# Attention, then a maxout FFN, on one core: one ring of five tiles for outputs and maxima, and new prices for transfers in the planner

## The chip, the cores and the metric

The kernel runs on one core of one Trainium2 chip. The metric is device microseconds of one launch, as the median of three runs: 785.98 us before the change (785.86 to 788.97).

## What is computed

```python
scores = scale * q @ k.T                        # 8 batches, 8 heads, 576 rows, head_dim 64, fp32
bias   = -(cum[:, None] - cum[None, :])         # cum = cumsum(max(s, 0)), per head
scores = where(causal, -1e9, scores + minimum(bias, 0))
attn   = softmax(scores); y = attn @ v          # then heads side by side: x is 4608 x 512
h      = max(x @ w1, x @ w2, x @ w3)            # w1, w2, w3: 512 x 768
out    = h @ w_out                              # w_out: 768 x 512
```

## The kernel before

Nothing in this program is written in the order in which an engine runs it. Every step (a group of matmuls, an eviction, a transfer) is added to a `Plan` with its buffers, a key (its rank) and, for each engine that may do it, a price in ns. `Plan.run` then plays the whole kernel through as a list scheduler with these prices, and the order in which it starts the steps is the order in which they are written for each engine's queue. On the chip each engine runs its queue in that order and waits in place for what a step needs. So a price is no delay by itself: it only decides which step stands ahead of which. A step with a number that is too low is placed too early, and its engine waits there.

**Prices.** A compute step is `(dur, busy)`: its result counts as there after `dur`, and its engine takes the next step after `busy`. A transfer has a third number, the time for which it fills the queue's DMA: in `Plan.run` its data counts as landed at `dma + dur`, where `dma = max(dma, now + busy) + third`. `load` prices a plain transfer at 450 ns of issue, its bytes at 0.3 (300 GB/s), and a latency of 2000 ns unless the call says otherwise. DMA transposes are priced where they are added, in `one_step` and `both`.

**Rings.** `depth` says how many tiles of a kind exist. `o` (two tiles) takes the scaled output of a down projection before its store; `m1` (three tiles) takes the running maximum of the three up projections. Both are "free" rings: a step that opens a tile waits in the plan until all steps of the tile that many places earlier have ended (`room`), its store among them, and the chip waits for the same.

**Work.** Batches come in units: "split" units (first 256 rows of a batch), "rest" units (the other 320 rows) and "whole" units. A unit loads `qr`, `rv` and the spread `bias`, then for each block of 128 rows masks (POOL), takes scores (PE), adds the bias and finds the minimum (DVE), takes the exponential (ACT), splits the result in two fp16 parts (ACT, DVE) and turns them with a DMA transpose issued from SP (lines 1299, 1107 and 1116); `values` multiplies by V. The heads of one (batch, row phase) make `x`, and `experts` then does the FFN as one set: 6 times three `u` groups of 12 matmuls with `m1` (L1479, L1490, L1502, L1509, L1514), then four `d` groups of 18 matmuls (L1535), each evicted by ACT into `o` (L1554) and stored from SP (L1560). Sets have the lowest rank on PE: they fill what attention leaves.

**The start.** The weights come as 64-bit words (L477) and are made into fp16 pairs in chunks of three or six by ACT, POOL and DVE (L485, L499, L506, L599, L637). Each chunk's scale is found with a gram matmul (L527), a reduction on DVE (L540), and `power`: a clip on DVE (L425), one matmul on PE (L434) and a reduction (L442). The first set (`first_set`, batch 0) uses the raw fp32 words (L659, L689).

Of the kernel before, what the change touches and what calls it, by code (L numbers as in the profile page):

```python
# [9 lines left out]
F32 = mybir.dt.float32  # L10
# [20 lines left out]
HOLD = (3000.0, 30000.0)  # L31
# [8 lines left out]
P3 = 10  # L40
LOWP = (2, 24)
# [30 lines left out]
class Plan:  # L72
# [48 lines left out]
    def run(self):  # L121
# [16 lines left out]
        while left:  # L138
# [4 lines left out]
            while events and events[0][0] <= now:  # L143
                _, _, _, op = heapq.heappop(events)
                if op is not None and op.start is None:
                    op.due = now + HOLD[0]
                    for e in op.ways:
                        heapq.heappush(wait[e], (op.key, op.n, op))
            for e in engines:
                if free[e] > now:  # L150
                    continue
                aside, pick, kept = [], None, None
                while wait[e]:
# [7 lines left out]
                    if kept is not None and op.mode:  # L161
                        break
                    if e == "PE" and op.mode and not shape and op.due > now > HOLD[1]:
                        kept = op
                        continue
                    pick = op
# [3 lines left out]
                if pick is None:  # L170
                    pick = kept
# [42 lines left out]
def kernel(  # L214
# [34 lines left out]
        qr=2, qh=2, ql=2, rv=4, vv=2, bias=2, p=2, pr=2, tl=2, pT0=2, pT1=2, tT=2, t=5, m1=3, o=2,  # L249
        sc=6, dg=2, am=3, vs=5, ws=3, os=4, s=2, av=1, m=3,  # L250
# [5 lines left out]
    for i in "abc":  # L256
# [3 lines left out]
        m1=1280, o=1280, sc=32, am=16, vs=32, ws=32, os=4,  # L260
# [55 lines left out]
    def load(emit, key, nbytes, reads=(), writes=(), queue="SP", rate=0.3, lat=2000.0, begin=0.0):  # L316
        plan.add({queue: (lat, 450.0, nbytes / rate * 1e-3)}, emit, key, reads, writes).ready = begin
# [20 lines left out]
    load(lambda e: E[e].dma_start(out=st()[0:HB], in_=s), -1000.0, 4 * HB * S, writes=[st], queue="ACT")  # L338
# [25 lines left out]
    def spans(c0, c1):  # L364
# [36 lines left out]
        lambda e: E[e].dma_start(out=cd(), in_=cct()[0:HB]), -1000.0, 4 * HB * S, [cct], [cd], queue="ACT", lat=5500.0  # L401
# [19 lines left out]
    def power(t, key):  # L421


        def do(e):
# [8 lines left out]
            {"PE": (250.0, 250.0)},  # L433
# [11 lines left out]


# [14 lines left out]

    def weights(c):
        ids = chunks[c]
        raw = {}
        for i in ids:
            k = (i if i < RAW else i - 1) % RAW
            if i == RAW:
# [123 lines left out]
        for i in ids:  # L591
# [4 lines left out]
            k = wkey(i)  # L596
# [46 lines left out]

    def first_set(c, raw):
# [4 lines left out]
        if c < NFT:  # L649
# [3 lines left out]
            for i in range(3):  # L653
                pm = buf("m", free=True, name=f"u_plain_{c}_{i}")
                r = raw[3 * c + i]

                def up(e, r=r, pm=pm):
                    for kt in range(NKT):
                        nc.tensor.matmul(  # L659
                            pm()[:, :nq], lhsT=words(r)[0][:, kt * P:(kt + 1) * P], rhs=xb()[:, kt * nq:(kt + 1) * nq],  # L660
                            start=(kt == 0), stop=(kt == NKT - 1),
                        )

                add({"PE": (NKT * cost + 100.0, NKT * cost)}, up, 1.0e6 + 3 * c + i, [r, xb], [pm])
                h = lambda: hb()[:, c * nq:(c + 1) * nq]
                if i == 0:
                    add(
                        {"ACT": act(nq, PSI), "DVE": dve(nq)},
                        lambda e, pm=pm, h=h: nc.scalar.activation(out=h(), in_=pm()[:, :nq], func=AF.Copy)
                        if e == "ACT"  # L670
                        else nc.vector.tensor_copy(out=h(), in_=pm()[:, :nq]),
                        FIRST + 3 * c, [pm], [(hb, c)],
                    )
                else:
                    add(
                        {"DVE": dve(nq, 155.0)},
                        lambda e, pm=pm, h=h: nc.vector.tensor_tensor(
                            out=h(), in0=pm()[:, :nq], in1=h(), op=ALU.max
                        ),
                        FIRST + 3 * c + i, [pm], [(hb, c)],  # L680
                    )
            return
        hb = H0[0]
        for dt in range(NDT):
            pm = buf("m", free=True, name=f"d_plain_{dt}")

            def down(e, pm=pm, dt=dt):
# [10 lines left out]
            o = buf("o", free=True, name=f"o_plain_{dt}")  # L698
# [9 lines left out]
                FIRST, 4 * P * nq, [o], lat=1500.0,  # L708
# [27 lines left out]
    def values_in(u):  # L736
# [19 lines left out]
        if plain(u):  # L756
            return
        first, last = gs[0] == 0, gs[-1] == NP - 1
        if first:
# [9 lines left out]
            k - 4.0, [rv], [(am, col)],  # L769
        )  # L770
        if last:
            vs = VS[sk] = buf("vs")
            kk = begin[u] - (1.0 if kind == "split" else 4.0)
# [5 lines left out]
            power(vs, kk)  # L779
# [52 lines left out]
    def qk_in(u):  # L832
# [98 lines left out]
        else:  # L931
            load(spread, k - LOOK[2], 4 * P * nb_ * rows_, [cd], [bias], lat=4500.0 if u < 4 else 2500.0)
# [85 lines left out]
    def both(u, t):  # L1018
# [94 lines left out]
        for tl, tT in zip(tls, tts):  # L1113
            add(
                {"SP": (2000.0, 1250.0, 200.0)},
# [76 lines left out]
    def one_step(u, a, g, qb, t, r, pT, sp, at):  # L1192
# [103 lines left out]
        tw = lambda n: (2000.0, 1250.0, 200.0 * n)  # L1296
# [8 lines left out]
    def turned(t, qb, pt, pr, sc, ri, pT, at):  # L1305
# [14 lines left out]
        for j in range(2):  # L1320
# [9 lines left out]
            add({"PE": (350.0 * (qb + 1) + 80.0, 350.0 * (qb + 1))}, turn, t, [(pt, (qb, j)), (pr, (qb, j))], [(m, j)])  # L1330
# [113 lines left out]

    def experts(b, ph, xb, vs):
# [73 lines left out]
        os = buf("os")  # L1519
        add(  # L1520
            {"DVE": (145.0, 65.0)},
            lambda e: nc.vector.tensor_scalar(
                out=os(), in0=vs()[:, 3:4], scalar1=ENDS()[:, 2:3], scalar2=None, op0=ALU.mult
            ),
            FIRST + 100.0 * n + 17, [(vs, 3), (ENDS, 2)], [os],
        )
        for dt in range(NDT):
            pm = buf("m", free=True, name=f"d{n}_{dt}")

            def down(e, pm=pm, dt=dt, f0=0, f1=NFT):  # L1530
                k = 3 * f0
                for ft in range(f0, f1):
                    v = W[NUP + ft]().rearrange("p h (a c) -> p h a c", c=P)
                    for wt, c in ((0, 0), (0, 1), (1, 0)):
# [93 lines left out]
```

## Time and profile before

| | us |
|---|---|
| median of 3 runs | 785.98 |
| profiled execution | 784.61 |
| its span, first to last instruction | 782.6 |
| PE busy in the span | 764.8 (98%) |
| DVE, ACT, POOL busy | 573.8, 519.2, 308.3 |
| DMA, mean rate | 174 GB/s, 136.31 MB in all |

The span is what the trace shows; 2.0 us lie around it. A row of a waits view names the waiting engine and line, and behind the arrow the step that ended its idle time.

### The profile page before, as it was taken

What the parts mean: (1) busy time and instruction counts of PE and PEld (TensorE: products, weight loads), DVE (VectorE), ACT (ScalarE), POOL (GpSimd) and SP (SyncE); (2) the same over time, 40 slices, a digit from 0 to 9 for tenths busy, and PEclk for the clock granted to TensorE, in tenths of its full rate; (3) what the DMA queues carried; (4) which work ended last, traced back from release to release, by engine and by line L of the source; (5) the groups of instructions that cost most, each with busy time, mean ns of one, the idle gap of its engine ahead of it and who ended that gap; (6) DMA issues with size and microseconds to landing.
All of it is one profiled execution on the core that took longest, in us unless ns stands there. A gap on an engine that the chain in (4) does not pass through costs nothing. (4 is left out here: it accounts for less than half of the span.)

```text
span 782.6 us, 19630 instructions
## 1 busy us (share of the span) xinstructions
PE 764.8 (98%) x7189; PEld 589.6 (75%) x7189; DVE 573.8 (73%) x1691; ACT 519.2 (66%) x1369; POOL 308.3 (39%) x361
## 2 busy tenths in 40 slices
PE   7889999999999999999999899999999999999998
PEld 5677888888888877766788677667776777778875
DVE  6999898875587888888878787888787977322131
ACT  6878777871687787986887777777876977111101
POOL 4432423641355455444544364354444452011110
PEclk9999999999999999999999999999999999999999
DMA  9799778890399899998999999898989865300000
GB/s 342 245 260 242 180 169 164 176 237 18 97 207 233 199 175 214 227 215 200 225 232 207 183 192 240 241 190 198 254 210 169 208 137 100 81 1 34 28 2 34
DMA packets 241167, 136.31 MB, mean 174 GB/s; under 512 B 204080, under 2 KB 222000, under 8 KB 241072
## 3 DMA queue, kind: packets, MB, share of 16 engines
q1 hardware_dynamic: 240912, 134.78, 75.7%
q8 instruction: 56, 0.92, 0.5%
q14 instruction: 39, 0.32, 0.2%
q10 hardware_dynamic: 160, 0.30, 0.1%
HBM read 75.64 MB, written 9.58 MB: 109 GB/s over the span
## 5 line engine op out<-in xcount | busy, mean ns | idle before, releaser
L1479 PE MATMUL u<-x,w 128*128 128x320 f16 (+1 forms) x3240 | 411.3, 287 | 2.9 <-ACT o L1554 2.9
L1479 PEld LDWEIGHTS <-w 128*128 128x128 f16 x3240 | 312.6, 98 | 99.5 <-issue 17.6
L1514 POOL TENSOR_TENSOR h<-m,h 128x320 f16<-128x320 f32 (+1 forms) x90 | 69.9, 777 | 190.4 <-ACT h L1509 174.5
L1535 PE MATMUL d<-h,w 128*128 128x320 f16 (+1 forms) x1080 | 137.9, 287 | 0.1
L1502 DVE SCALAR_TENSOR_TENSOR m<-u,m 128x320 f32<-128x320 f32 (+1 forms) x180 | 82.2, 457 | 64.3 <-PE u L1479 60.1
L1535 PEld LDWEIGHTS <-w 128*128 128x128 f16 x1080 | 104.7, 98 | 30.4 <-issue 3.2
L1222 POOL TENSOR_SCALAR_AFFINE_SELECT p<-bias 128x256 f32<-128x256 f32 (+3 forms) x91 | 68.9, 770 | 120.6 <-DVE pr L1288 68.9
L1244 ACT ACTIVATE p<-p,sc 128x256 f32<-128x256 f32 (+3 forms) x182 | 98.2, 540 | 26.3 <-DVE sc L1235 25.6
L1509 ACT ACTIVATE h<-m 128x320 f16<-128x320 f32 (+1 forms) x90 | 39.4, 438 | 102.9 <-DVE m L1502 102.6
L1288 DVE SCALAR_TENSOR_TENSOR pr<-p,sc,pr 128x256 f16<-128x256 f32 (+3 forms) x182 | 100.3, 567 | 8.0 <-ACT pr L1280 7.8
L1280 ACT ACTIVATE pr<-p,sc 128x256 f16<-128x256 f32 (+3 forms) x182 | 89.3, 538 | 13.0 <-DMA pT<-pr 7.9
L961 POOL TENSOR_TENSOR ql<-qr,qh 128x256 fp32r<-128x256 f32 (+1 forms) x76 | 82.5, 1106 | 35.0 <-ACT qh L949 30.6
L1235 DVE CUSTOM_DVE_ANT_0 p<-s,p 128x256 f32<-128x256 f32 (+3 forms) x182 | 80.4, 467 | 3.7 <-POOL p L1222 2.2
L1384 PEld LDWEIGHTS <-vv 128*64 128x64 f16 x1232 | 58.6, 110 | 18.1 <-issue 10.0
L1384 PE MATMUL av<-pT,vv 128*64 128x320 f16 (+3 forms) x1104 | 70.3, 276 | 1.2 <-DVE x L1429 0.8
L1494 DVE TENSOR_SCALAR m<-u 128x320 f32<-128x320 f32 (+1 forms) x55 | 25.3, 461 | 48.2 <-PE u L1479 47.6
L1554 ACT ACTIVATE o<-d,os 128x320 f32<-128x320 f32 (+1 forms) x60 | 28.2, 498 | 47.6 <-PE d L1535 36.8
L766 DVE TENSOR_REDUCE am<-rv 128x1 f32<-128x640 f32 (+1 forms) x44 | 33.9, 777 | 13.2 <-DMA rv<-in_qkv_dram 13.0
L1222 POOL TENSOR_SCALAR_AFFINE_SELECT ha<-bias 128x1024 f32<-128x1024 f32 (+3 forms) x29 | 26.7, 926 | 41.8 <-DVE r L1288 29.8
L1244 ACT ACTIVATE ha<-ha,sc 128x512 f32<-128x512 f32 (+3 forms) x58 | 35.9, 620 | 6.5 <-DVE sc L1235 6.1
L815 DVE SCALAR_TENSOR_TENSOR vv<-rv,vs,vv 128x640 f16<-128x640 f32 (+1 forms) x44 | 39.0, 887 | 0.4
L1288 DVE SCALAR_TENSOR_TENSOR r<-ha,sc,r 128x512 f16<-128x512 f32 (+3 forms) x58 | 37.5, 660 | 2.3 <-ACT r L1280 2.2
(170 smaller groups left out, 980.1 us busy)
## 6 DMA issues: line engine op xcount, KB each, us to landing
bias<-cd SPq DMA_DIRECT2D x32, 576.0 KB, 5.0
qr<-in_qkv_dram SPq DMA_DIRECT2D x28, 480.0 KB, 5.2
rv<-in_qkv_dram SPq DMA_DIRECT2D x32, 320.0 KB, 3.8
raw<-in_w_dram SPq DMA_DIRECT2D x16, 512.0 KB, 5.7
qr<-in_qkv_dram SPq DMA_DIRECT2D x13, 512.0 KB, 6.3
bias<-cd SPq DMA_DIRECT2D x12, 512.0 KB, 5.4
out_dram<-o SPq DMA_DIRECT2D x32, 160.0 KB, 2.4
early<-in_w_dram SPq DMA_DIRECT2D x8, 512.0 KB, 7.0
```

The lines of the kernel that those rows point to most:

```text
L961: lambda e, d0=d0, d1=d1: E[e].tensor_tensor(out=lo().bitcast(F32R)[:, d0:d1], in0=raw()[:, d0:d1], in1=hi()[:, d0:d1], op=ALU.subtract),
L1222: nc.gpsimd.affine_select(out=pt()[:, 0:8 * P].rearrange("p (j n) -> p j n", j=2)[:, :, at:at + nk], in_=r["bias"]()[:, 2 * a * w:2 * (a + ...
L1235: lambda e, j=j: nc.vector.tensor_tensor_reduce(out=pj(j), in0=src(j), in1=pj(j) if masked else bias(j), scale=-SCALE, scalar=3.0e38, op0= ...
L1244: lambda e, j=j: nc.scalar.activation(out=pj(j), in_=pj(j), func=AF.Exp, scale=-1.0, bias=nm()[:, j:j + 1], accum_out=sm()[:, j:j + 1]),
L1280: lambda e, h_=h_, s_=s_, j=j: nc.scalar.activation(out=h_(), in_=s_(), func=AF.Copy, scale=ri()[:, j:j + 1]),
L1288: lambda e, h_=h_, l_=l_, s_=s_, j=j: nc.vector.scalar_tensor_tensor(out=l_(), in0=s_(), scalar=ri()[:, j:j + 1], in1=h_(), op0=ALU.mult, ...
L1384: nc.tensor.matmul(av()[j * D:(j + 1) * D, c0:nq], lhsT=lt, rhs=rt, start=(n < 2), stop=(n >= len(todo) - 2), skip_group_check=True,)
L1479: nc.tensor.matmul(pm()[:, :nq], lhsT=v[:, wt, kt, :], rhs=x(xt, kt), start=(k == 0), stop=(k == 3 * NKT - 1),)
L1502: lambda e, pm=pm, m1=m1: nc.vector.scalar_tensor_tensor(out=m1()[:, :nq], in0=pm()[:, :nq], scalar=HSC, in1=m1()[:, :nq], op0=ALU.mult, o ...
L1509: lambda e, m1=m1, ft=ft: nc.scalar.activation(out=h(0, ft), in_=m1()[:, :nq], func=AF.Copy),
L1514: lambda e, m1=m1, ft=ft: E[e].tensor_tensor(out=h(1, ft), in0=m1()[:, :nq], in1=h(0, ft), op=ALU.subtract),
L1535: nc.tensor.matmul(pm()[:, :nq], lhsT=v[:, wt, dt, :], rhs=h(c, ft), start=(k == 0), stop=(k == 3 * NFT - 1), skip_group_check=True,)
```

## The change

`o` is dropped: outputs use the ring `m1`, which is five tiles deep instead of three. The tiles keep their size, so the two kinds together take what they took before. A further ring `far` of one tile of 512 bytes is made but not used.

Transfers have new prices. Each price has now a fourth number, the time from issue to the start of the transfer (`lead`), which takes the place of the issue time in the landing, and every transfer issued through `load` and every transpose has 1500 ns (`SPARE`) added to its latency. A plain load goes from 450 + bytes/0.3 + 2000 to 1440 + bytes/0.36 + 1285 + 1500; an output store from 450 + bytes/0.3 + 1500 to 120 + bytes/0.45 + 1320 + 1500; the spread bias from 450 + bytes/0.3 + 2500 to 1590 + bytes/0.266 + 1065 + 1500. A transpose of n blocks goes from 1250 + 200 n + 2000 to 545 + 156 n + 1570 + 1500, and holds SP for 1200, 1450 or 2000 ns instead of 1250. On PE, `power`'s matmul goes from 250 to 90 ns of engine time, and the turns of the first units from 350 to 270 ns a block.

What else the diff adds is not run at the values that stand in it: `RAWX`, `D16`, `KP` and `LATE` are 0, `FAR` is 99 with 46 units, `SAME` is 0, and `HOLD2` would start at 900 us. With `SAME` 0 and a third number of 2 the new loop over PE's held steps picks as the old one does. `down_all` is the old text of the down projection, moved.

```diff
-HOLD = (3000.0, 30000.0)
+HOLD = (3000.0, 30000.0, 2)
+SAME = 0
+D16 = 0
+SPARE = 1500.0
+FAR = 99
...
                 if len(op.ways[e]) > 2:
-                    dma[e] = max(dma[e], now + busy) + op.ways[e][2]
+                    dma[e] = max(dma[e], now + op.ways[e][3]) + op.ways[e][2]
                     op.end = dma[e] + dur
...
-        qr=2, qh=2, ql=2, rv=4, vv=2, bias=2, p=2, pr=2, tl=2, pT0=2, pT1=2, tT=2, t=5, m1=3, o=2,
-        sc=6, dg=2, am=3, vs=5, ws=3, os=4, s=2, av=1, m=3,
+        qr=2, qh=2, ql=2, rv=4, vv=2, bias=2, p=2, pr=2, tl=2, pT0=2, pT1=2, tT=2, t=5, m1=5,
+        sc=6, far=1, dg=2, am=3, vs=5, ws=3, os=4, s=2, av=1, m=3,
...
-    def load(emit, key, nbytes, reads=(), writes=(), queue="SP", rate=0.3, lat=2000.0, begin=0.0):
-        plan.add({queue: (lat, 450.0, nbytes / rate * 1e-3)}, emit, key, reads, writes).ready = begin
+    def load(emit, key, nbytes, reads=(), writes=(), queue="SP", rate=0.36, lat=1285.0, begin=0.0, lead=1440.0):
+        plan.add({queue: (lat + SPARE, 400.0, nbytes / rate * 1e-3, lead)}, emit, key, reads, writes).ready = begin
...
         add(
-            {"PE": (250.0, 250.0)},
+            {"PE": (250.0, 90.0)},
             lambda e: nc.tensor.matmul(
                 gm()[:, :P], lhsT=t()[:, 1:2].bitcast(BF16)[:, 0:1].to_broadcast([P, P]), rhs=identb(), start=True,
...
-            load(spread, k - LOOK[2], 4 * P * nb_ * rows_, [cd], [bias], lat=4500.0 if u < 4 else 2500.0)
+            load(spread, k - LOOK[2], 4 * P * nb_ * rows_, [cd], [bias], lat=3000.0 if u < 4 else 1065.0, rate=0.266, lead=1590.0)
...
-                {"SP": (2000.0, 1250.0, 1600.0)},
+                {"SP": (1570.0 + SPARE, 1250.0, 1250.0, 545.0)},
...
-                {"SP": (2000.0, 1250.0, 200.0)},
+                {"SP": (1570.0 + SPARE, 1200.0, 156.0, 545.0)},
...
-        tw = lambda n: (2000.0, 1250.0, 200.0 * n)
+        tw = lambda n: (1570.0 + SPARE, 1200.0 if n < 10 else 1450.0 if n < 14 else 2000.0, 156.0 * n, 545.0)
...
-            add({"PE": (350.0 * (qb + 1) + 80.0, 350.0 * (qb + 1))}, turn, t, [(pt, (qb, j)), (pr, (qb, j))], [(m, j)])
+            add({"PE": (270.0 * (qb + 1) + 80.0, 270.0 * (qb + 1))}, turn, t, [(pt, (qb, j)), (pr, (qb, j))], [(m, j)])
...
+            o = buf("m1", free=True, name=f"o{n}_{dt}")
...
+            load(
+                lambda e, o=o, dt=dt: nc.sync.dma_start(out=outT[dt * P:(dt + 1) * P, t0:t0 + nq], in_=o()[:, :nq]),
+                FIRST, 4 * P * nq, [o], lat=1320.0, lead=120.0, rate=0.45,
+            )
```

## Rows read from the trace of the kernel before

**Rows 1.** Busy time of each engine in six stretches of the span (length, then busy us and instructions of PE, PE's weight loads, DVE, ACT and POOL, granted PE clock as a share of 2.4 GHz, DMA share, GB/s), with the sum.

```profile
0.00:20.00 20.00, 16.01 (x145) 10.64 (x145) 14.03 (x58) 13.95 (x45) 9.07 (x22) 1.00 0.95 343
20.00:120.00 100.00, 93.51 (x1007) 78.20 (x1005) 91.13 (x328) 78.58 (x226) 35.32 (x50) 1.00 0.86 213
120.00:420.00 300.00, 300.00 (x2920) 239.95 (x2918) 238.68 (x707) 222.05 (x601) 137.31 (x157) 1.00 0.87 188
420.00:520.00 100.00, 96.71 (x901) 70.60 (x894) 80.66 (x209) 75.52 (x177) 47.28 (x48) 1.00 0.98 211
520.00:660.00 140.00, 139.31 (x1266) 98.84 (x1265) 117.44 (x323) 107.70 (x274) 65.78 (x68) 1.00 0.85 189
660.00:782.00 122.00, 119.22 (x973) 91.38 (x971) 31.82 (x72) 21.40 (x48) 13.49 (x18) 1.00 0.13 33
sum 782.00, PE 764.75 PEld 589.61 DVE 573.76 ACT 519.21 POOL 308.26; mean PE 127.46 PEld 98.27 DVE 95.63 ACT 86.53 POOL 51.38
```

**Rows 2.** Pieces of the chain that ended last, near the end of the span: start, length, what (matmuls in the piece).

```profile
708.66 23.58 PE u L1479 x216
...
740.10 29.34 PE u L1479 x216
769.44 9.79 PE d L1535 x72
779.30 0.53 ACT o L1554
```

**Rows 3.** What PE waited for, over the whole span: total us, times, longest.

```profile
PE m L434 <- DVE ws L425: 3.4, 3, 1.8
PE u L1479 <- ACT o L1554: 2.9, 2, 2.1
PE m L415 <- DVE identb L361: 1.6, 1, 1.6
PE m L434 <- DVE vs L425: 1.0, 2, 0.6
PE u_plain L659 <- PE m L434: 0.9, 1, 0.9
PE av L1384 <- DVE x L1429: 0.8, 1, 0.8
...
PE m L434 <- DVE vs L776: 0.5, 1, 0.5
PE av L1384 <- DMA pT<-pr: 0.3, 1, 0.3
PE m L434 <- ACT o L1554: 0.3, 1, 0.3
```

**Rows 4.** All instructions on tile `o`: what ACT's evictions (L1554) waited for, who waited for them, and the stores' time to landing.

```profile
  PE d L1535: 36.8, 25
  DMA out_dram<-o: 8.8, 6
...
DMA to landing us min/median/max: 1.7/2.5/5.0
```

**Rows 5.** Timeline around the longer of the two PE waits: start, length, engine, line, operation.

```profile
440.51 0.86 SPq L1560 DMA_DIRECT2D out_dram<-o  x2
...
442.18 1.20 PE L1030 MATMUL s<-qr 64*64 64x256 f32 x16
...
444.97 0.84 ACT L1554 ACTIVATE o<-d,os 128x256 f32<-128x256 f32 x2 [3.65 <-DMA out_dram<-o]
...
445.49 3.42 PE L1479 MATMUL u<-x,w 128*128 128x320 f16 x24 [2.11 <-ACT o L1554]
```

**Rows 6.** Timeline around the shorter one, with SP's queue between the first two evictions and their stores.

```profile
491.67 0.95 ACT L1554 ACTIVATE o<-d,os 128x320 f32<-128x320 f32 x2 [1.02 <-PE d L1535]
492.82 0.99 SPq L753 DMA_DIRECT2D rv<-in_qkv_dram  x2
...
493.91 2.67 SPq L1299 DMA_TRANSPOSE pT<-r  x1
...
496.67 1.12 SPq L1560 DMA_DIRECT2D out_dram<-o  x2
...
499.37 0.53 ACT L1554 ACTIVATE o<-d,os 128x320 f32<-128x320 f32 x1 [1.25 <-DMA out_dram<-o]
...
499.95 0.22 PE L434 MATMUL m<-identb,vs 128*128 128x128 bf16 x1 [0.26 <-ACT o L1554]
...
500.97 1.25 PE L1479 MATMUL u<-x,w 128*128 128x320 f16 x8 [0.81 <-ACT o L1554]
```

**Rows 7.** DMA issues by destination: count, KB each, median us from issue to landing.

```profile
bias<-cd SPq DMA_DIRECT2D x32, 576.0 KB, 5.0
rv<-in_qkv_dram SPq DMA_DIRECT2D x32, 320.0 KB, 3.8
raw<-in_w_dram SPq DMA_DIRECT2D x16, 512.0 KB, 5.7
...
pT<-pr SPq DMA_TRANSPOSE x115, 4.7
```

**Rows 8.** The weight loads (L477): issue and landing (min/median/max), and who waited for them.

```profile
  POOL raw L499: 11.0, 4
  ACT early L485: 6.7, 5
  POOL early L499: 3.9, 2
...
DMA to landing us min/median/max: 3.6/6.0/9.1
```

**Rows 9.** PE groups by shape: count, then busy us, mean ns of one, and idle time before them. (The chip runs an fp32 matmul of the program as two instructions.)

```profile
L434 PE MATMUL m<-identb,vs 128*128 128x128 bf16 x14 | 3.1, 223 | 1.2 <-DVE vs L425 1.0 <-ACT o L1554 0.3
...
L1324 PE MATMUL m<-pr-8_287,p-8_238 128*128 128x128 f32 x12 | 1.9, 292 | 0.7 <-ACT bias L926 0.7
...
L1324 PE MATMUL m<-pr-2_481,p-2_427 128*128 128x128 f32 x12 | 1.6, 284 | 0.0
L434 PE MATMUL m<-identb,ws 128*128 128x128 bf16 x7 | 1.6, 225 | 4.0 <-DVE ws L425 3.4 <-DVE vs L776 0.5
```

**Rows 10.** One stretch of `u` matmuls between other PE work, in the timeline: start, length, count.

```profile
319.06 6.69 PE L1479 MATMUL u<-x,w 128*128 128x320 f16 x48
```

More of the change, by code (lines that the diff above doesn't have):

```diff
@@ L145, in run @@
                 if op is not None and op.start is None:
-                    op.due = now + HOLD[0]
+                    op.due = now + (HOLD2 if now > HOLD2[1] else HOLD)[0]
                     for e in op.ways:
@@ L160, in run @@
                         continue
[L161 to L164, printed above, removed]
+                    if e == "PE" and op.mode:
+                        kept.append(op)
+                        if shape and (op.mode == shape or not SAME):
+                            pick = op
+                            break
+                        if not shape and (len(kept) >= (HOLD2 if now > HOLD2[1] else HOLD)[2] or not op.due > now > HOLD[1]):
+                            pick = kept[0]
+                            break
                         continue
-                    pick = op
+                    pick = kept[0] if kept and shape else op
                     break
@@ L336 @@
     cct = inner("cc", 12 * S, 4 * S)
-    load(lambda e: E[e].dma_start(out=st()[0:HB], in_=s), -1000.0, 4 * HB * S, writes=[st], queue="ACT")
+    load(lambda e: E[e].dma_start(out=st()[0:HB], in_=s), -1000.0, 4 * HB * S, writes=[st], queue="ACT", lat=2000.0)
     def do(e):
@@ L400 @@
     load(
-        lambda e: E[e].dma_start(out=cd(), in_=cct()[0:HB]), -1000.0, 4 * HB * S, [cct], [cd], queue="ACT", lat=5500.0
+        lambda e: E[e].dma_start(out=cd(), in_=cct()[0:HB]), -1000.0, 4 * HB * S, [cct], [cd], queue="ACT", lat=4000.0
     )
@@ L443, in power, with far_power @@
             key, [gm], [(t, 2)],
+        )
+    def far_power(t, key, n):
+        fd = Buf(plan, f"far{n}", lambda b: dram.tile([P, 1], F32, name=f"far{n}"), "one")
+        row = buf("far", name=f"far_row{n}")
+        add(
+            {"DVE": (157.0, 75.0)},
+            lambda e: nc.vector.tensor_scalar(
+                out=t()[:, 1:2], in0=t()[:, 0:1], scalar1=2.0 ** -80, scalar2=1.0 / VSC, op0=ALU.max, op1=ALU.mult
+            ),
+            key, [(t, 0)], [(t, 1)],
+        )
+        load(lambda e: E[e].dma_start(out=fd(), in_=t()[:, 1:2]), key, 4 * P, [(t, 1)], [fd], rate=1.0e-3)
+        load(
+            lambda e: E[e].dma_start(out=row(), in_=fd().rearrange("p o -> o p").to_broadcast([P, P])),
+            key, 4 * P * P, [fd], [row],
+        )
+        add(
+            {"DVE": (282.0, 200.0)},
+            lambda e: nc.vector.tensor_reduce(out=t()[:, 2:3], in_=row(), axis=AX.X, op=ALU.max),
+            key, [row], [(t, 2)],
         )
@@ L466, in weights @@
             k = (i if i < RAW else i - 1) % RAW
-            if i == RAW:
+            if RAWX:
+                k = RAWAT[i]
+            if RAWX and i > RAW and k < 0:
+                r = buf("ql" if k == -1 else "qh", name=f"raw{i}")
+            elif i == RAW:
                 r = Buf(plan, "r6", lambda b: early3()[:, 0:2 * N], "one", inside=early3)
@@ L697, in first_set @@
             )
-            o = buf("o", free=True, name=f"o_plain_{dt}")
+            o = buf("m1", free=True, name=f"o_plain_{dt}")
             add(
@@ L755, in values_in @@
         sk = (b, kind)
-        if plain(u):
+        if plain(u) and not D16:
             return
@@ L768, in values_in @@
             ),
-            k - 4.0, [rv], [(am, col)],
+            AMK if plain(u) else k - 4.0, [rv], [(am, col)],
         )
@@ L778, in values_in @@
             )
-            power(vs, kk)
+            if u >= FAR:
+                far_power(vs, kk - 1.0, u)
+            else:
+                power(vs, kk)
             add(
@@ L1518, in experts @@
             )
[L1519 to L1534, printed above, removed]
[L1535 to L1562 removed]
+        down_all(n, t0, nq, hb, h, vs, base)
     gone = 0
```

166 lines of the change are left out of this document (119 added, 47 removed).

## Prediction

> **What bounds the kernel now.** I read the busy time by stretches first, because the stages differ. [rows 1] show PE busy for 764.75 of 782 us at full granted clock, so 17.8 us of the 782.6 us span are open. They lie in three places: 4.0 us in the first 20 us and 6.5 us from 20 to 120, where DVE is busy for 91.13 of 100 us; nothing from 120 to 420; 3.3 us from 420 to 520 and 0.7 us from 520 to 660; and 2.8 us from 660 on, plus the last 0.6 us, which are the tail. The second thing to see is whether a busy PE is a full PE. At the end, where nothing competes, 216 matmuls of 256 columns take 23.58 us and 216 of 320 columns 29.34 us [rows 2]: 109.2 and 135.8 ns each, against 106.7 and 133.3 ns for as many columns at 2.4 GHz. The change adds and removes no matmul, so this part stays; only the 17.8 us and the switches between kinds of PE work can move.
>
> Third, what PE waited for [rows 3]. The waits fall in two families. One is of the start: 3.4 us for the clip of a weight chunk's maximum, 1.6 us for the identity, and some pieces below 1 us. The other is an eviction of outputs, 2.9 us for `u` and 0.3 us for `power`'s matmul, all of it between 440 and 501 us. Fourth, why that eviction was late. ACT's evictions into `o` waited 8.8 us in six cases for a store to land [rows 4]. In the longer case [rows 5] two stores go out at 440.51, PE ends its scores at 443.4, ACT has sat idle for 3.65 us until a store has landed, evicts at 444.97, and PE goes on with `u` after 2.11 us of idleness (its PSUM tile was still held). In the shorter [rows 6] the evictions end at 492.6, but SP issues two loads and a transpose of 2.67 us before the stores, at 496.67; the next eviction waits 1.25 us and PE, soon after, 0.8 us and 0.3 us.
>
> **The change, part by part.** All terms are against the profiled execution: 782.6 us of span and 784.61 us in all.
>
> *The ring of five.* In a ring of two an output opens when the store two places earlier has landed. Two `d` groups are 36 matmuls, 3.9 us (256 columns, 36 x 109.2 ns) or 4.9 us (320 columns); the eviction takes half a us and the store 2.5 us at the median but 5.0 at most [rows 4], and SP can hold it for 4.0 us (492.62 to 496.67, [rows 6]). So the ring breaks whenever SP is late. In the ring of five, the four outputs of a set take tiles of maxima long read, and the tile of the first output is opened again by the second maximum of the next set: three `d` groups (5.9 us), one `u` group (12 x 109.2 ns, 1.3 us) and three more (3.9 us) later, some 11.1 us. The worst seen, 0.5 + 4.0 + 5.0 = 9.5 us, fits. The maxima had three tiles and have five between outputs, so they lose nothing. I take all of it, 2.9 + 0.3 = **-3.2 us**; the bounds are 0 (something else holds the same PSUM tile as long) and -3.2. ACT was idle before these evictions and the `d` groups had ended, which is why I take the far end.
>
> A rule of the Trainium skill speaks against this reading. Perfetto Trace Analysis, section Optimization Strategy, says that a bubble which repeats over a stretch on the engine that should be saturated can mean too few buffers. Here six of 60 evictions waited, and two reached PE, which is no repeating gap; by the rule the ring would not be the limit, this term would be 0 and the sum 1.1 us. The direct row (an eviction released by its own ring's store) is what I go by, and the other case is rival two.
>
> *The prices of loads.* A weight load of 512 KB counted as landed 0.45 + 1.75 + 2.0 = 4.20 us after issue, and now 1.44 + 1.46 + 2.79 = 5.68 us; recorded are 6.0 at the median, 9.1 at most [rows 8]. `rv` goes from 3.54 to 5.14 (recorded 3.8), the bias from 4.92 to 6.37 (recorded 5.0) [rows 7]. The old prices were close to or below the median, so about half of the readers stood too early. Nothing on the chip starts later by this: a load goes out as soon as its tile is free. What moves is the reader's place in its engine's queue: behind others that are ready. From 120 us on these waits sit on engines that have room (DVE 238.68 of 300, [rows 1]) and PE has FFN work in reserve; that reserve is visible in the stretch from 660 on, where PE is the only busy engine. I cost it at 0 there, covered by that reserve; without cover it is 1.5 us per load, in a chain that PE waits for.
>
> *The prices of transposes.* For 8 blocks 4.85 against 4.86 us, for 16 blocks 6.45 against 6.11, recorded 4.7 at the median over all sizes [rows 7]. They hardly move. One wait of PE for a transpose, 0.3 us [rows 3], stands for what is left; with one more wait of 0.3 us for `power` I take **-0.3 us** for the middle, bounds -0.6 and +1.2 (one new wait of each of the sizes seen, 0.8 and 0.3). SP's own time for large transposes rises from 1250 to 2000 ns in the plan; the 2.67 us of [rows 6] is still above it. SP runs what stands in its queue in order, so behind a transpose that waits for its input stand stores and loads; the plan places them better, not surely.
>
> *The prices on PE at the start.* `power`'s matmul is recorded at 0.22 us from start to end [rows 9], and the plan held PE for 0.25 us by it; now for 0.09, since the next matmul may follow into the pipeline. Some 21 of them (14 and 7 in the groups by shape) made PE 3.4 us slower in the plan. The turned blocks go from 0.35 to 0.27 us; six of them take 1.6 to 1.9 us in the trace, 0.27 to 0.32 each [rows 9]. A PE that is slower in the plan than on the chip comes early to a matmul that needs DVE, and waits there. From 20 to 120 us PE waited five times at L434 itself (three times for `ws`, twice for `vs`, [rows 3]); shortened by 0.16 us each, the part of the price that was too much, this is **-0.8 us**. Bounds: half of the 6.5 us of idleness there either way, -3.2 and +3.2, since a new order brings new meetings of PE and DVE that this trace does not show.
>
> *Switches and tail.* PE's switches between kinds of work may rise or fall a little; one stretch of 48 matmuls of 320 columns among other work takes 6.69 us [rows 10], 0.17 us over 48 x 135.8 ns. A new order has no reason to bring more or fewer such stretches; I take 0, and for the bounds five of them, -0.8 and +0.8. The tail is the last eviction (0.53 us, [rows 2]) and a store of 2.5 us: unchanged, there is one output in flight.
>
> Sum: -3.2 - 0.3 - 0.8 = **-4.3 us**. The profiled execution would be 780.3 us, its span 778.3. The runs have a median 1.4 us above the profiled one, and I put the difference on it: 785.98 - 4.3 = **781.7 us**.
>
> **The rivals.**
>
> *One: the start gains too.* If the 6.5 us of idleness from 20 to 120 us halve (-3.2) and switches fall (-0.8), with the ring (-3.2) and the middle at its good end (-0.6), the sum is -7.8 us: 778.2. For it: 14.9 us of POOL's and 6.7 of ACT's waits there are for weight loads [rows 8], and later-placed readers free those engines. Against: DVE, not these, is what PE waits for [rows 3].
>
> *Two: the ring is not the limit.* SP's lateness stays, the freed ACT runs into the next late thing (the PSUM tile of the next `d`, a load on DVE), and PE waits as long at the same place. Then only -1.1 us are left: 784.9. For it: in [rows 6] the stores were late at the issue. Against: a later store is harmless once nobody waits for its tile.
>
> *Three, slower: the reserve costs the weights.* Each of eight chunks of weights is read 1.48 us later in the plan (5.68 - 4.20), DVE fills the time with attention, and the chunk's scale, for which PE waits, comes later on the chip as well. All uncovered it is 8 x 1.48 = 11.8 us, less the 3.5 us of the first two terms: +8.3, 794.3 us. It makes the kernel slower by over 0.5% (3.9 us) where more than (3.5 + 3.9) / 11.8 = 63% is uncovered. For it: DVE is busy for 91% of that stretch [rows 1]. Against: the recorded median landing of 6.0 us [rows 8] is later than even the new price, so the readers move to where the data is. The Trainium skill's page DMA: Bandwidth & Descriptors, section Anatomy of one DMA, has, for transfers issued from GpSimd, a fixed 2.0 us plus bytes at 436 GB/s, an estimate of 3.2 us for 512 KB; by it the old price already had a reserve and this rival would be likelier. The measured landings decide against it.
>
> *Four: the plan hardly moves* and the time stays at 786.0.
>
> **How the numbers follow.** The forecast, with its own range 780.0 to 783.5, has 0.56; rival one 0.15; two 0.16; three 0.09; four 0.04. A difference of 0.5%, 3.9 us, is about what a measurement of this kernel can tell from none. Of the forecast's 0.56, the part beyond 3.9 us (782.05 and below) is 0.35 and the rest 0.21. Faster is 0.35 + 0.15 = 0.50, same 0.21 + 0.16 + 0.04 = 0.41, slower 0.09. The range reaches from 777.5, below rival one's 778.2 and about where the bounds' good ends meet, to 786.3, above rivals two and four; it leaves out rival three and little else.
>
> **What would show it.** In the changed profile: no eviction L1554 waits for `out_dram<-o`, and no PE wait names ACT `o` (term one); PE busy from 120 to 660 us is within 1 us of full (terms one and two); PE busy stays near 764.8 us; waits of PE for `ws` and `vs` between 20 and 120 us come down so that PE's idle time there is 5.7 us in place of 6.5 (term three); waits of DVE, POOL and ACT for `rv` and weight loads shrink. It would be wrong if PE's idle time from 20 to 120 us grew by several us, or if PE busy moved by more than 1 us, which would mean that switches count for more than I allow.

## The result, and the profile after

The changed kernel is slower: 792.21 us at the median (789.87 to 794.7, 8 runs) against 785.92 us for the kernel before (783.86 to 790.13, 8 runs), a ratio of 1.0068 with a 95% interval of 1.0039 to 1.0096. I had forecast 781.7 us, faster by 4.3, and the time lies above my range. Its profiled execution took 789.87 us, with a span of 788.0 us against 782.6.

The busy time by stretches of the changed kernel (columns as in [rows 1]):

```profile
0.00:20.00 20.00, 12.89 (x64) 8.28 (x65) 9.31 (x35) 9.05 (x29) 5.87 (x15) 0.88 0.94 330
20.00:120.00 100.00, 93.80 (x1041) 78.42 (x1041) 95.51 (x343) 80.46 (x233) 35.86 (x53) 0.99 0.79 214
120.00:420.00 300.00, 299.77 (x2904) 239.46 (x2903) 231.26 (x694) 222.73 (x604) 137.04 (x155) 1.00 0.85 184
420.00:520.00 100.00, 96.98 (x910) 71.90 (x909) 81.82 (x210) 71.75 (x168) 46.73 (x47) 1.00 0.96 210
520.00:660.00 140.00, 139.42 (x1269) 99.01 (x1268) 122.54 (x324) 108.59 (x273) 71.05 (x73) 1.00 0.90 195
```

Against [rows 1], PE's idle time in the first 20 us goes from 4.0 to 7.1 us; from 20 to 120 it is 6.2 in place of 6.5; from 120 to 660 it is 3.8 in place of 4.0. PE busy over the span grows from 764.8 to 767.2 us, with the same matmuls. So 3.1 us of idleness and 2.4 us of longer matmuls make the 5.4 us, and both belong to the start. The middle, where I looked for 3.5 us of gain, gave 0.2.

What PE waited for, over the whole span (answering to [rows 3]):

```profile
PE s-2_291 L1250 <- DVE sc L1336: 5.0, 1, 5.0
PE u L1627 <- DVE m L1650: 2.2, 1, 2.2
PE u_plain L743 <- DVE raw L548: 1.8, 1, 1.8
PE m L429 <- DVE identb L375: 1.6, 1, 1.6
```

One wait of 5.0 us is new at the top, and the waits for ACT's eviction of `o` are gone. The first leads back from PE to DVE, POOL and ACT, and stands in ACT's queue. ACT's timeline of the first 15 us:

```profile
7.21 0.69 ACT L527 ACTIVATE early<-raw 128x512 f32<-128x512 f32 x1 [4.41 <-DMA raw<-in_w_dram]
7.79 0.60 ACT L1027 ACTIVATE bias<-m 128x512 f32<-128x512 f32 x1
13.08 0.48 ACTq L415 DMA_DIRECT2D cd<-early  x1
13.61 0.66 ACT L527 ACTIVATE early<-raw 128x512 f32<-128x512 f32 x1 [5.22 <-DMA rv<-in_qkv_dram]
14.17 1.07 ACT L1027 ACTIVATE bias<-m 128x512 f32<-128x512 f32 x2
```

ACT ends the first eviction of `bias` at 8.4 us. Next in its queue is the transfer of the cumulated sums to `cd`, and that is not issued before 13.08. Its data were there: DVE wrote them at 7.8. The releaser is a load of `rv`, which the transfer has nothing to do with. The list of waits of the built programs tells why. Each transfer of SP and ACT signals its landing on one of eight semaphores (DMAHW0 to 7), taken in turn, and the next transfer on the same semaphore is first made to wait until the one before it has landed. Changed kernel and kernel before, ACT's queue:

```
5 L1027 ACTIVATE bias0_233<-m_1_223 128x512 [waits PE_49]
6 L415 DMA cd_236<-early_165 64x576 [waits DMAHW0_49,DVE_49]
7 L527 ACTIVATE early_165<-raw1_190 128x512 [waits DMAHW4_49]

5 L401 DMA cd_226<-early_165 64x576 [waits DMAHW2_49,DVE_49]
6 L926 ACTIVATE bias0_229<-m_1_218 128x512 [waits PE_49]
7 L926 ACTIVATE bias0_229<-m_2_223 128x512 [waits PE_49]
```

Before, `cd` stood ahead of the evictions, was given semaphore 2, and waited for the second `qr` load, long landed; it went out at 7.6 us. Now it stands behind one eviction, comes later in the rotation, and waits on semaphore 0 for the first `rv`, issued at 4.96 us into a DMA that is full at that time (a share of 1.02 to 1.05 from 5 to 20 us). PE runs out of work meanwhile. Timeline of PE and then the stretches of 5 us:

```profile
10.80 0.93 PE L1250 MATMUL s-4_275<-qr 64*128 64x128 f32 x8 [0.49 <-DVE sc L1336]
...
16.68 1.65 PE L1250 MATMUL s-2_291<-qr 64*128 64x128 f32 x8 [4.96 <-DVE sc L1336]
```

```profile
10.00:15.00 5.00, 1.23 (x10) 0.52 (x8) 0.74 (x4) 1.39 (x3) 0.18 (x1) 1.00 1.05 382
15.00:20.00 5.00, 3.32 (x16) 2.67 (x17) 3.71 (x16) 5.00 (x23) 3.04 (x5) 0.50 1.05 368
20.00:25.00 5.00, 3.97 (x28) 3.38 (x29) 4.46 (x20) 3.63 (x13) 3.84 (x7) 0.82 0.60 207
```

While PE stands, from 11.7 to 16.7 us, the granted clock falls: it is 1.00 from 10 to 15 us and 0.50 of 2.4 GHz, the lower level of 1.2, from 15 to 20. Eight score matmuls take 1.65 us there where as many took 0.93 before the pause. At the lower level half of the busy time is extra: half of 3.32 us, and, as 0.82 is a mix of 64% at the higher level and 36% at the lower, 18% of 3.97 us. That is an estimate of 2.4 us, the growth of PE busy.

In the middle, the evictions of `o` waited for a store once (8.8 us in six cases before, [rows 4]):

```profile
  DMA out_dram<-o: 1.9, 1
```

yet PE lost 2.19 us at 424 to 426 us. The timeline there:

```profile
418.30 2.97 SPq L1217 DMA_TRANSPOSE tT<-tl  x2
...
421.37 0.99 SPq L851 DMA_DIRECT2D rv<-in_qkv_dram  x2
...
425.13 0.82 DVE L864 TENSOR_REDUCE am<-rv 128x1 f32<-128x640 f32 x1 [2.23 <-DMA rv<-in_qkv_dram]
...
425.87 0.41 DVE L1650 SCALAR_TENSOR_TENSOR m<-u,m 128x256 f32<-128x256 f32 x1
...
426.33 1.47 PE L1627 MATMUL u<-x,w 128*128 128x256 f16 x12 [2.19 <-DVE m L1650]
```

SP issues two transposes for 2.97 us, then two loads of `rv`. DVE stands at the maximum of the first until it lands, 3.8 us after its issue, and behind that in DVE's queue is the eviction (L1650) that frees PE's PSUM tile. In the kernel before, DVE stood for `rv` as well, until 444.53 us, at the place of the longer PE wait of [rows 5]:

```profile
444.53 0.82 DVE L766 TENSOR_REDUCE am<-rv 128x1 f32<-128x640 f32 x1 [2.37 <-DMA rv<-in_qkv_dram]
```

There the store, on which ACT stood until 444.97, was the last to come; here it is `rv`. Whether this wait took the place of the stores' is what e5, e9 and e10 below ask.

### The profile page after: what moved, and what is told of

It reads as the page before. It is cut to its first block, busy times and chain, and to the rows that moved or that the text cites. A ratio compares the mean times of both kernels' runs of the same rounds, so it can differ in the third digit from the quotient of the medians.

```text
span 788.0 us, 19642 instructions
## 1 busy us (share of the span) xinstructions
PE 767.2 (97%) x7189; PEld 592.0 (75%) x7189; DVE 578.1 (73%) x1694; ACT 518.8 (66%) x1366; POOL 311.5 (40%) x361
## 5 line engine op out<-in xcount | busy, mean ns | idle before, releaser
L1323 POOL TENSOR_SCALAR_AFFINE_SELECT p<-bias 128x256 f32<-128x256 f32 (+3 forms) x91 | 70.5, 786 | 135.4 <-DVE pr L1389 65.3
L1650 DVE SCALAR_TENSOR_TENSOR m<-u,m 128x320 f32<-128x320 f32 (+1 forms) x180 | 81.9, 455 | 53.7 <-PE u L1627 48.5
L1389 DVE SCALAR_TENSOR_TENSOR pr<-p,sc,pr 128x256 f16<-128x256 f32 (+3 forms) x182 | 102.2, 578 | 8.1 <-ACT pr L1381 7.9
L1485 PEld LDWEIGHTS <-vv 128*64 128x64 f16 x1232 | 59.1, 110 | 18.0 <-issue 11.1
L1642 DVE TENSOR_SCALAR m<-u 128x320 f32<-128x320 f32 (+1 forms) x63 | 28.6, 455 | 52.4 <-PE u L1627 51.6
L1050 ACT ACTIVATE qh<-qr 128x896 fp32r<-128x896 f32 (+1 forms) x40 | 38.9, 972 | 6.5 <-DMA qr<-in_qkv_dram 6.1
L864 DVE TENSOR_REDUCE am<-rv 128x1 f32<-128x640 f32 (+1 forms) x44 | 33.6, 773 | 11.1 <-DMA rv<-in_qkv_dram 11.1
L1381 ACT ACTIVATE r<-ha,sc 128x512 f16<-128x512 f32 (+3 forms) x58 | 33.0, 619 | 12.1 <-DMA pT<-r 7.6
```

The source lines that it names most:

```text
L1323: nc.gpsimd.affine_select(out=pt()[:, 0:8 * P].rearrange("p (j n) -> p j n", j=2)[:, :, at:at + nk], in_=r["bias"]()[:, 2 * a * w:2 * (a + ...
L1381: lambda e, h_=h_, s_=s_, j=j: nc.scalar.activation(out=h_(), in_=s_(), func=AF.Copy, scale=ri()[:, j:j + 1]),
L1389: lambda e, h_=h_, l_=l_, s_=s_, j=j: nc.vector.scalar_tensor_tensor(out=l_(), in0=s_(), scalar=ri()[:, j:j + 1], in1=h_(), op0=ALU.mult, ...
L1485: nc.tensor.matmul(av()[j * D:(j + 1) * D, c0:nq], lhsT=lt, rhs=rt, start=(n < 2), stop=(n >= len(todo) - 2), skip_group_check=True,)
L1650: lambda e, pm=pm, m1=m1: nc.vector.scalar_tensor_tensor(out=m1()[:, :nq], in0=pm()[:, :nq], scalar=HSC, in1=m1()[:, :nq], op0=ALU.mult, o ...
```

## The experiments

Theory one: the loss is the place of the transfer of `cd` in ACT's queue. Theory two (my rival three): the reserve puts readers too late. Theory three: the ring's gain in the middle is taken up by DVE standing for `rv`. A ratio is to the kernel before on the same chip, with a 95% interval; PE idle is worked out from the stretches of each profile.

### Undoing and doing the swap: e1, e2

```diff
 e1, the changed kernel: Plan.write puts cd (and DVE's steps for it) ahead of the ACT step before it
+        at = max(k for k in range(cd) if seq[k].eng == "ACT")
+        part = seq[at:cd + 1]
+        seq[at:cd + 1] = [o for o in part if o.eng == "DVE" or o is part[-1]] + [
+            o for o in part if o.eng != "DVE" and o is not part[-1]]
 e2, the kernel before: cd behind the next ACT step
+        at = min(k for k in range(cd + 1, len(seq)) if seq[k].eng == "ACT")
+        seq.insert(at, seq.pop(cd))
```

> The changed kernel with one pair swapped in ACT's queue: the transfer of cd (L415) stands before the first eviction of bias (L1027) again, as in the kernel before; every other engine's order is that of the changed kernel. Theory one (the whole loss comes from this transfer, which in the changed kernel waits at the head of ACT's queue until 13.1 us for another transfer): ACT's 5.2 us wait and PE's 5.0 us wait in the first 20 us go, PE keeps its full clock there, the span falls by about 5.3 us to 782 to 784, and the time is 0.997 to 1.002 of the kernel before. Theory two (the reserve on all transfers puts the readers of weights and loads too late): the span stays within 1.5 us of 788.

> The kernel before with the same pair swapped the other way: the transfer of cd behind the first eviction of bias. Theory one: the transfer now waits for a weight load of 512 KB that lands at about 11 us, so ACT stands for some 3 us at the start, the span grows by 2 to 4 us (785 to 787), and nothing else changes. Theory two: no price is touched, so the time stays that of the kernel before within 0.3%.

e1: 1.0021 (0.9998 to 1.0045), span 784.4. ACT's timeline, then the first 20 us:

```profile
7.74 0.48 ACTq L422 DMA_DIRECT2D cd<-early  x1
8.26 0.60 ACT L1034 ACTIVATE bias<-m 128x512 f32<-128x512 f32 x1 [0.42 <-issue]
8.75 0.67 ACT L534 ACTIVATE early<-raw 128x512 f32<-128x512 f32 x1
```

```profile
0.00:20.00 20.00, 15.91 (x98) 10.42 (x99) 14.73 (x63) 13.85 (x46) 9.99 (x23) 1.00 0.94 338
```

The transfer goes out at 7.74, PE is busy for 15.9 of 20 us at full clock, and the span falls by 3.6 us, where theory one said 5.3. The rest lies far behind the start. e1's PE is idle for 17.7 us of its span, as before (17.8), but busy for 766.7 us in place of 764.8: after a wait for DVE, which had stood for `rv` for 3.26 us, this stretch ran in part at the lower clock.

```profile
PE u L1634 <- DVE m L1657: 2.1, 1, 2.1
420.00:440.00 20.00, 19.51 (x192) 14.89 (x192) 17.87 (x44) 14.53 (x32) 9.78 (x11) 0.91 0.94 222
```

e2: 1.0039 (1.0016 to 1.0063), a median of 789.15 us. The execution in its profile (793.33 us, span 791.4) is the slowest of its twelve, so its span overstates the cost; the median less the 2.0 us around a span gives 787.2, at the upper end of what was expected. Its ACT queue:

```profile
8.17 0.60 ACT L930 ACTIVATE bias<-m 128x512 f32<-128x512 f32 x1 [0.28 <-PE m L922]
11.09 0.48 ACTq L405 DMA_DIRECT2D cd<-early  x1
11.62 0.60 ACT L930 ACTIVATE bias<-m 128x512 f32<-128x512 f32 x1 [2.86 <-DMA raw<-in_w_dram]
```

The kernel before, with old prices and old rings, shows the same stop when this one pair is swapped: until 11.09 us, for the weight load that now comes up on that semaphore. No engine's order but that of this one place is changed in either run (with it, the few SP transfers in between come up on another semaphore), so the cause is shown, in both directions. Two later pairs with and without the swap (e14 against e11, e4 against e15) repeat the sign.

### The two halves apart: e3, e4

```diff
 e3, the kernel before
-        ... t=5, m1=3, o=2,
+        ... t=5, m1=5,
-            o = buf("o", free=True, ...)
+            o = buf("m1", free=True, ...)      (and the first set's outputs likewise)
 e4, the changed kernel: the same lines the other way
```

> The kernel before with the ring of five alone, all prices old. My term for the ring: no eviction L1554 waits for a store, PE's 3.2 us of waits for ACT o go, the start is that of the kernel before, span 779 to 780, ratio 0.996. The rival (what is late next takes the place): stores are not waited for, yet PE loses 2 to 3 us elsewhere between 420 and 520 us, span 782 to 783, ratio 0.999 to 1.001. If the loss came from the ring: span above 786.

> The changed kernel with the two rings of before (o two deep, m1 three), all prices new. Theory one: the start is that of the changed kernel, with ACT's wait to 13 us, and the span is about 788 plus what the stores' waits cost, 0 to 3 us: 787 to 791, ratio 1.005 to 1.01. Theory two: the same time, so this run alone does not tell the two apart; it tells whether the ring had any part in the loss, in which case it would be at 783 or below.

e3: 1.0002 (0.998 to 1.0024), span 782.5. No store is waited for, and PE waits elsewhere:

```profile
PE m L434 <- DVE ws L425: 3.8, 3, 1.8
PE m L434 <- DVE vs L425: 3.3, 4, 1.6
```

My term for the ring failed here; the rival of the expectation has its number. `vs` comes from the maxima of the loaded values, for which DVE waited 10.4 us. e4: 1.0073 (1.0047 to 1.0099), span 790.1, with ACT standing until 13.48 us: the ring had no part in the loss.

### DVE's wait for the values taken away: e5, e9, e10

These kernels leave out the scale of V in the units named, so their output is another.

```diff
 all rest and whole units, in the kernels of e1 (e5), before (e9) and e3 (e10)
-                out=am()[:, col:col + 1], in_=rv()[:, 0:n], axis=AX.X, ...
+                out=am()[:, col:col + 1],
+                in_=rv()[:, 0:n] if kind == "split" else W[0]().rearrange("p a n -> p (a n)")[:, 0:n],
```

> The kernel of e1 (changed prices and ring, the pair in ACT's queue swapped back) in which the maxima of the values (L864 in the changed kernel) of all rest and whole units are taken from a tile of weights that has long been in place, not from the loaded values: so the scale of V is left out for these units and the output is another. The order on every engine is that of e1; only DVE's wait for the rv loads at these reductions is gone. Theory three (what took the place of the waits for stores is DVE, standing in its queue for rv loads that SP issued late): PE's idle time from 120 to 660 us falls from 4.1 us to 1.5 us or less, the span from 784.4 to 781 to 782.5, the ratio to 0.995 to 0.999. The rival (the values are read by ACT and DVE soon after, so the wait only moves on to their split): idle time stays at 3 us or more and the span at 783.5 or more.

> The kernel before, in which the maxima of the values of all rest and whole units are taken from a tile of weights in place of the loaded values, as in e5 (the scale of V is left out for these units). Order unchanged on every engine. Theory three: DVE's 13 us of waits for rv go, but PE was held there by stores, not by these: its 3.2 us of waits for the eviction of outputs stay at 2 us or more, and the span falls by 1.5 us at most, to 781 to 782.6, ratio 0.997 to 1.0. The rival: the stores' waits were themselves pushed by DVE (SP's and DVE's queues run late together), they go as well, and the span falls to 779 or less without any ring.

> The kernel of e3 (ring of five, old prices) with the maxima taken from the weights as in e9. Theory three: the 3.3 us that PE waited for the maxima of the values in e3 go and the ring shows its worth: span 782.5 to 779 or 780, ratio 0.993 to 0.997, below e9 by 1.5 us or more. The rival: the ring is worth nothing, and e9 and e10 come out within 0.7 us of each other.

e5: 0.9974 (0.9953 to 0.9995), span 781.4, against e1's 1.0021; PE idle from 120 to 660 us 2.3 us against 4.1, and the granted clock from 420 to 520 us 1.00 against 0.98. That is between the two theories' bounds, nearer to theory three. e9: 1.0001 (0.9978 to 1.0024); DVE's waits for `rv` fall from 13.0 to 1.7 us, while those of ACT for stores are 10.4 us (8.8 before) and PE's for ACT `o` 2.6 (3.2 before), so the stores' waits don't hang on DVE's. The span, 785.2, went up rather than down. e10: 0.9989 (0.9971 to 1.0008), span 781.0. The profiles differ by 4.2 us as theory three asks, the medians by 0.8 (786.17 and 785.34), within both intervals. So the wait for `rv` costs under the new prices; that it hid the ring under the old ones is not shown by these times.

### The reserve, and cd from another queue: e6, e7, e8

```diff
 e6, the changed kernel             e7, the kernel of e1
-SPARE = 1500.0                    -SPARE = 1500.0
+SPARE = 0.0                       +SPARE = 3000.0
 e8, the changed kernel
-    ... [cct], [cd], queue="ACT", lat=4000.0
+    ... [cct], [cd], lat=4000.0
```

> The changed kernel with SPARE 0, so the new prices without the reserve. The plan then places the transfer of cd ahead of the evictions by itself. Theory one: the start is again that of the kernel before (PE busy for 16 of the first 20 us), and the span is within 2 us of e1's 784.4. Theory two (the reserve costs the readers time): beyond the start it gains too, below 782. If the reserve is worth what it was meant for, more engines stand for loads and PE's idle time from 120 to 660 us is above e1's 4.1 us, with a span of 786 or more.

> The kernel of e1 with a reserve of 3000 ns in place of 1500. Theory three: the readers of rv stand later, DVE's 12.2 us of waits for rv fall by half or more, PE's idle time from 120 to 660 us falls below e1's 4.1 us, the span comes to 781 to 783. Theory two: every further ns costs; the span is 786 or more, with the growth from 20 to 120 us.

> The changed kernel with the transfer of cd issued from SP's queue in place of ACT's. Theory one: what cost the time is that ACT's queue stood behind this transfer, not the transfer itself; ACT goes on at 8.4 us, PE's 5.0 us wait in the first 20 us is gone or below 1 us, and the span is 783 to 786. If the late data of cd is what counts, or the order of the other steps, the span stays at 787 or more.

e6: 1.0155 (1.0133 to 1.0177), span 794.9. Without the reserve the plan puts `cd` ahead of the evictions by itself: it goes out at 7.92 us, and PE is idle for 3.1 of the first 20 us. So it is the reserve that had moved it. The kernel is slower still, with 9.9 us of PE idle from 20 to 120 us and 5.8 from 120 to 660, so theory two finds no support; e1, which keeps the reserve and loses the stop, had already shown that the reserve's other effects are not the main loss. e7: 1.0033 (1.0016 to 1.005), span 786.4: DVE's waits for `rv` fall from 12.2 to 3.7 us as theory three said, but PE idle in the middle only to 3.6 us, and from 20 to 120 us it grows from 5.7 to 6.7. e8: 1.011 (1.0089 to 1.0132), span 793.0. ACT goes on at 9.4 us (8.4 expected), and the time is worse all the same. ACT's and SP's timeline, then the stretches:

```profile
9.40 0.68 ACT L527 ACTIVATE early<-raw 128x512 f32<-128x512 f32 x1
```

```profile
13.30 0.52 SPq L415 DMA_DIRECT2D cd<-early  x1
```

```profile
0.00:20.00 20.00, 16.23 (x88) 10.47 (x88) 12.80 (x52) 11.06 (x36) 8.98 (x21) 0.91 0.93 332
20.00:120.00 100.00, 91.57 (x1015) 75.64 (x1017) 93.61 (x335) 76.85 (x222) 30.05 (x48) 0.98 0.77 205
120.00:420.00 300.00, 297.58 (x2870) 236.67 (x2866) 229.84 (x686) 220.54 (x597) 135.67 (x154) 0.99 0.85 186
```

PE's start is good, though `cd` goes out at 13.30 us, later than in the changed kernel: in the first 20 us it is ACT's stop that costs, and not the late data of `cd`. PE then loses 8.4 us from 20 to 120 and 6.8 from 120 to 660. One edit to a queue changed the order of the whole kernel, and the new order costs more than the stop it removed. So beyond the first 20 us e6, e7 and e8 say what their kernels take, but not by which of the many changed orders; that is left open.

### The loads of rv ranked earlier: e11 to e14, e15, e16

```diff
 rest and whole units, in the kernels of e1 (e11), e3 (e12), before (e13), changed (e14), e15 (e16)
-                ... out=rv(), in_=qkv[b, gs[0], :, V0:QKV]), k - LOOK[1], ...
+                ... out=rv(), in_=qkv[b, gs[0], :, V0:QKV]), k - 12.0, ...
 e15: the kernel of e1 with the old rings (the lines of e4)
```

> The kernel of e1 with the rv loads of rest and whole units ranked 8 steps earlier on SP (rank k - 12 in place of k - 4); nothing is left out. Theory three: DVE's 12.2 us of waits for rv fall, PE's idle time from 120 to 660 us goes from 4.1 to 2.5 us or less, span 781 to 783, ratio 0.996 to 0.999. If the wait is set by the tile (a load can't start before the split of V four units earlier) rather than by SP's order, DVE's waits stay above 8 us and the span within 1 us of 784.4.

> The kernel of e3 (ring of five, old prices) with the same earlier rank for the rv loads; nothing is left out. Theory three: PE's 3.3 us of waits for the maxima of the values fall below 1.5 us, span 780 to 781.5, ratio 0.995 to 0.999: a kernel ahead of both. If the tile sets the wait, it stays at e3's time, ratio 0.999 to 1.002.

> The kernel before with the rv loads of rest and whole units ranked 8 steps earlier on SP; old prices, old rings. If the earlier rank alone makes the gain of e11 and e12, the ratio is 0.995 to 0.998 here too, span 779.5 to 781. If it gains only where stores don't hold the rings, stores go on to stop ACT (8 us or more of waits) and the ratio is 0.998 to 1.001, and e12 against this run is what the ring is worth.

> The changed kernel with the same earlier rank for rv, and the transfer of cd left behind the eviction. Theory one: the start costs what it cost in the changed kernel, 4 to 5.5 us against e11, whatever the middle does: ratio 0.999 to 1.003, PE busy for less than 14 of the first 20 us. If the start were made up for later, the ratio would be e11's 0.995.

> The kernel of e1 (new prices, pair swapped back) with the two rings of before. Against e1 (1.0021) it gives the ring's worth under the new prices. My term says 3.2 us, so 1.005 to 1.007 here; the rival (the ring's waits hand over to others) says within 0.15% of e1.

> The kernel of e11 (new prices, pair swapped back, rv ranked earlier) with the two rings of before. Against e11 (0.9949) it gives the ring's worth where rv is not in the way. If the ring pays once rv is out of the way: 0.998 or more, with 5 us or more of ACT waits for stores. If not: within 0.15% of e11.

| prices | cd first | ring of five | rv as it was | rv earlier |
|---|---|---|---|---|
| old | yes | no | 1 (before) | 0.9969 (0.9946 to 0.9991), e13 |
| old | no | no | 1.0039, e2 | |
| old | yes | yes | 1.0002, e3 | 0.9964 (0.9945 to 0.9984), e12 |
| new | yes | no | 1.0001 (0.998 to 1.0022), e15 | 1.0013 (0.9992 to 1.0034), e16 |
| new | yes | yes | 1.0021, e1 | 0.9949 (0.9928 to 0.9971), e11 |
| new | no | yes | 1.0068, changed kernel | 1.0024 (1.0004 to 1.0044), e14 |
| new | no | no | 1.0073, e4 | |

Down the columns: `cd` in second place costs 0.47% (e1 to the changed kernel), 0.75% (e11 to e14), 0.72% (e15 to e4) and, under the old prices, 0.39% (the kernel before to e2): 3.1 to 5.9 us, four times the same sign. e14's start shows it by itself: PE busy for 13.6 of 20 us, one wait of 4.8 us, and then no idle time of PE at all from 420 to 660. The granted clock of the first 20 us falls in each pair too: from 1.00 to 0.88, 0.91 to 0.83, 0.91 to 0.78 and 1.00 to 0.90.

The ring gains -0.02 (e3), +0.05 (e13 to e12), -0.20 (e15 to e1), +0.64 (e16 to e11) and, without the swap, +0.05% (e4 to the changed kernel); the pair of e9 and e10 gives +0.12. The mean is 0.1%, 0.8 us, and all of it is the one pair that is clear of its intervals: the other five give 0.0. By its expectation that pair, e16 to e11, speaks for a ring that pays once `rv` is out of the way. But of the 7.5 us that ACT waits for stores in e16's profile 0.3 us reach PE, and the same pair under the old prices gives 0.05%, so the ring is not shown to be what makes its 0.64%.

The new prices with the swap undone gain between -0.44% (e13 to e16) and +0.15% (e12 to e11). The earlier rank gains 0.31 to 0.72% in four of five pairs and loses 0.12 in one (e15 to e16). DVE's waits for `rv` fell in e13 (7.9 us from 13.0) and e14 (7.6 from 11.1), hardly in e11 (10.3 from 12.2) and not in e12 (13.6 from 10.4), so I can't say that it works by them alone. The profiles of e11 (786.15 us) and e16 (789.58) are each of the slowest of that kernel's twelve runs, so what they show of the middle may not be what the median run does.

e11 is ahead of both kernels: 781.96 us at the median (778.98 to 786.15), 0.5% below the kernel before and 1.2% below the changed one.

## Why the prediction was wrong

**The step that failed** is the one on the prices of loads. I wrote that nothing on the chip starts later by a price, that what moves is the reader's place, and costed it at 0 with PE's reserve of FFN work as cover. I went through SP's queue only. The two transfers of ACT's queue carry the reserve too: in the plan `s` lands at 1.44 + 0.41 + 3.5 = 5.35 us in place of 2.94, `cd` is ready later than the first eviction, and so it stands behind it. And a transfer can start later by its place: it waits for its turn of eight semaphores. There was no FFN work for PE at 12 us, so there was no cover; the price was 3.1 us of idleness and 2.4 us of halved clock in the profile, 3.7 to 5.9 us by the runs under the new prices. In the kernel before, ACT's queue already stood for 3.9 us there, for the first weight load.

**The ring, -3.2 us.** The first half of the mechanism was right: the stores' waits fell from 8.8 to 1.9 us, and PE waits no more for ACT's `o`. The second half, that PE gains this time, was wrong: six pairs of runs lie between -0.20 and +0.64%, and five of them give 0.0 together. I had reasoned that ACT was idle and the `d` groups done, so that nothing was late behind the store. DVE was: its queue stood for `rv` at the same places (until 444.53 and 495.98 us in the kernel before), and PE waits for whichever is last. Rival two, with 784.9 us, described this middle, and it named a load on DVE as what would be late next; that the wait for `rv` is what ate the gain is supported by e5 and not shown by e9 and e10. The Trainium skill (Perfetto Trace Analysis, section Optimization Strategy) takes a gap that repeats over a stretch as a possible sign of too few buffers. Two single waits are no such gap, and e3's 1.0002 agrees better with that than with my reading of the row.

**The middle, -0.3 us:** PE's idle time from 120 to 660 us, terms one and two together, fell by 0.2 us in place of 3.5. **The start's prices on PE, -0.8 us:** idle time from 20 to 120 us fell by 0.3, within what a new order does. **Switches, 0:** PE busy without the estimated 2.4 us of halved clock is 764.8 us, as before. **The tail** is as forecast, with the last eviction at 0.53 us and 0.3 us more behind it. **The clock** was in no term: I had taken PE's 1.00 for given, and it fell in the changed kernel.

**Rival three** had the sign, but not the mechanism: it said that readers of weights come too late, with PE idle from 20 to 120 us; that stretch did not grow, and without the reserve (e6) the kernel is slower. Its 1.48 us for each chunk also left out that loads queue behind each other in the plan, each for 1.46 us now and 1.75 before, so that every load ahead takes 0.29 us of it back. **Rival one** did not happen.

What stays open: why one new order has 0.5 us of PE idle in the middle (e14) and another 8.1 (e16, in its slowest run), what makes the pair of e16 and e11, and how the earlier rank of `rv` gains.

## What to carry to other kernels

When a planner's prices change, follow every queue that carries one of them from the first instruction on, the short ones first: one transfer in an engine's queue stops that engine for as long as it can't be issued, and PE with it where PE has no reserve of work yet. A wait that ends on one engine is worth only the time until the next queue that is late at the same place; look at who else stands there before taking the whole wait as gain. And to test a cause in a kernel whose order is planned, swap the one pair after planning: an edit ahead of the planner brings another order, whose own differences (here 0.9 and 1.3%, e8 and e6 against e1) are larger than the effect.

## What the runs showed of the hardware

A transfer issued from ACT waited 4.7 us, with its data ready, for a load of SP's queue to land, because both use the same one of eight completion semaphores; the load itself took 8.0 us from issue (4.96 to 13.0 us) while the DMA moved 382 to 388 GB/s.

A pause of PE of 5.0 us went with a granted clock of 0.50 for the stretch from 15 to 20 us and 0.82 for the next, though PE was busy for 3.3 and 4.0 of the 5 us: some 2.4 us in slower matmuls on top of the 3.1 us by which idle time grew. The length of a wait alone did not tell whether the clock falls. A wait of 2.10 us in e1 was followed by 0.91 from 420 to 440 us, one of 2.19 us at the same `u` matmuls of the changed kernel by 1.00; and e15 has 0.91 in its first 20 us, where no wait of PE behind its first matmul is longer than 1.1 us.
